# Attention and two feed-forward layers in one kernel: later pairs' keys and queries are transposed in the values' idle PSUM bank, and the way-in is reordered

## The chip, the cores and the metric

One core of a Trainium2 chip runs the whole program. The time is device microseconds of one execution, from its start to its end. TensorE (PE) multiplies matrices into PSUM, eight banks of 512 fp32 columns on 128 partitions; VectorE (DVE) and ScalarE (ACT) read PSUM; GpSimd (POOL) works from SBUF to SBUF; SyncE (SP) issues the DMAs. Each engine runs its own instructions in order and waits on semaphores.

## The reference

Inputs are q, k and v of 4 batches x 8 heads x 576 rows x 64 columns.

```
q, k = rotate(q), rotate(k)             # rotary embedding
attn = softmax(q @ k.T / sqrt(64))      # per head, 576 x 576
x    = (attn @ v)                       # heads side by side: 2304 x 512
x    = (sigmoid(x @ w_gate) * (x @ w_val)) @ w_out     # 512 -> 1536 -> 512
out  = elu(x @ w_in) @ w_out2                          # 512 -> 2048 -> 512
```

## The kernel before, in words

The 32 heads are taken one after the other, two heads being a *pair* (16 pairs). A head has a *slot* of `NSTEP` = 10 steps: five for the first 288 query columns (half a = 0), five for the second, each step being one block of keys (four of 128 rows and one of 64). In a step PE computes, in this order, the scores `s` of this block (two products, of high and low parts of fp32 numbers), up to two products `mt` whose row maxima belong to the head two slots later, and the product `pv` of exponentials `e` and values that is five steps old. So the values of a head's first half run in steps 5 to 9 of its slot, those of its second half (`pv_1`) in steps 0 to 4 of the next slot.

ACT takes the exponentials; DVE takes the maxima `MX` of each `mt`, subtracts the rounded part of the last block (`p<-s,p`, `low_part`) and copies the finished values `u` out of PSUM (`evacuate`). Once per head the maxima are joined (`MJ`), turned by PE (`mr`) and sent by DMA (`W<-row`) into the operands `W` of the next head.

PSUM has three rings of banks: `ps_mt` (3 banks, maxima), `ps_qk` (3 banks, scores and `mr`) and `ps_pv` (2 banks, values). The two banks of `ps_pv` go to the two halves of a head in turn, so the bank of `pv_1` is free from the copy of its values in the middle of a slot to step 0 of the next.

Keys and queries are prepared a few slots ahead, a pair at a time. POOL rotates them (`rope_ops`: `rk`, `rq`, and `rt`, the last 64 rows of both). `split` has PE transpose them into a PSUM tile `T`, ACT copy the rounded part (`hl<-T`, "high") and DVE subtract it from `T` (`hl<-T,hl`, "low"). `move` sends the parts by DMA into `W`.

The order is written by hand: `at(slot, step, fn)` puts work on an agenda. In the main loop the agenda of step h - 0.5 runs first, then scores, maxima and values of step h, then the agenda of step h. What a function emits there goes to the end of each engine's queue. For pair `pr` and `s0 = 2*pr`, keys of pair 4 and later are split in slot s0-5 (an odd slot), queries in slot s0-4 (an even one). In an odd slot no `mt` runs at steps 8 and 9; in an even one it does.

From slot 5 on, `split_w` converts the first weights of the feed-forward layers: a piece of it is pulled at steps 2 and 5 of each slot (lines 122 to 143: integer work on DVE, copies on ACT, differences on POOL).

`inverse` takes the reciprocal of the softmax sums in parts: sums to DRAM, back as 128 x 9 (`r<-d`), reciprocal on DVE, back to DRAM (`d<-r`), and out to 64 rows (`rb<-d`); `normalized` multiplies on POOL.

The feed-forward layers follow at 302 us and are not touched.

Of the kernel before, what the change touches and what calls it, by code (L numbers as in the profile page):

```python
# [9 lines left out]
F32 = mybir.dt.float32  # L10
F32R = mybir.dt.float32r
AF = mybir.ActivationFunctionType
ALU = mybir.AluOpType
# [7 lines left out]
def attention_moe_moe_kernel(  # L21
# [15 lines left out]
    nc = tc.nc  # L37
    B, H, S, D = q.shape
    P = 128
    NT, DM = out.shape  # L40
    NPAIR = B * H // 2
# [4 lines left out]
    SM = ST * P  # L46
    TL = S - SM
    HS = S // 2
    HM = SM // 2
# [136 lines left out]
    with ExitStack() as att:  # L186
# [10 lines left out]
        ps_mt = banks.enter_context(tc.tile_pool(name="ps_mt", bufs=3, space=bass.MemoryType.PSUM))  # L197
        ps_qk = banks.enter_context(tc.tile_pool(name="ps_qk", bufs=3, space=bass.MemoryType.PSUM))
        ps_pv = banks.enter_context(tc.tile_pool(name="ps_pv", bufs=2, space=bass.MemoryType.PSUM))
# [36 lines left out]
        first = [raw_p.tile([P, n, 2, D * n], F32, tag=nm, name=f"{nm}0") for nm, n in (("k", ST // 2), ("q", ST // 2))]  # L236
        raws["k", 0] = first[0].rearrange("p a h x -> p (a h x)").rearrange("p (h t d) -> p h t d", h=2, d=D)
        raws["q", 0] = first[1].rearrange("p a h x -> p (a h x)").rearrange("p (a h t d) -> p a h t d", a=2, h=2, d=D)
        for j in range(2):
            nc.sync.dma_start(  # L240
                out=raws["k", 0][:, j].rearrange("p t d -> p (t d)"),
# [3 lines left out]
                out=tab[:, 1 - j].rearrange("p t d -> p (t d)"),  # L245
                in_=rope_main[:, 1, 1 - j].rearrange("p t d -> p (t d)"),
            )
        for j, queue in enumerate((nc.sync, nc.scalar)):
            queue.dma_start(
                out=raws["q", 0][:, j].rearrange("p h t d -> p h (t d)"),  # L250
# [62 lines left out]
        def at(slot, step, fn, *args):  # L313
            agenda.setdefault(slot * NSTEP + step, []).append((fn, args))

        rot = {}
# [51 lines left out]

        parts = {}

        def split(pr, which, half, pool, tag, low=None):

            if which == "k" and half == 0:

                parts[pr] = hl_p.tile([P, 4, S], F32R, tag="hl", name=f"hl{pr}")
            tails = which == "k" and half == 1
            c0, n = half * HM, HM + (P if tails else 0)
            T = pool.tile([P, 512], F32, tag=tag, name=f"T{which}{pr}_{c0}")[:, 0:n]
            rows = [rot[pr, which][:, c // P] for c in range(c0, c0 + HM, P)] + ([rot[pr, "t"]] if tails else [])
            for j, r in enumerate(rows):  # L380
                nc.tensor.transpose(T[:, j * P : (j + 1) * P], r.rearrange("p h d -> p (h d)"), ident)  # L381
            c0 += 0 if which == "k" else S + TL
            hi, lo = (parts[pr][:, 2 * j : 2 * j + 2].rearrange("p w s -> p (w s)")[:, c0 : c0 + n] for j in range(2))
            high = lambda: nc.scalar.copy(hi, T)
            rest = lambda: nc.vector.tensor_tensor(out=lo, in0=T, in1=hi.bitcast(F32), op=ALU.subtract)
            if low is None:
                high()
                rest()
            else:
                slot, step = low  # L390
                at(slot, step - 1, high)
                at(slot, step, rest)

        def move(pr, ab):

# [24 lines left out]
        def bank(pr, key, pool, tag):  # L420
            if (pr, key) not in banks_of:
                banks_of[pr, key] = pool.tile([P, 512], F32, tag=tag, name=f"T{key[0]}{key[1]}_{pr}")
            return banks_of[pr, key]
# [26 lines left out]
        def high(pr, key):  # L450
            T, hi, lo = way_in[pr, key]
            nc.scalar.copy(hi, T)
# [141 lines left out]
        def values(i, h):  # L594


            a, t = divmod(h, ST + 1)
            pr, ab = divmod(i, 2)
            par = pr % 2
            c = slice(a * HS, (a + 1) * HS)  # L600
            if t == 0:
                ps[i, a] = ps_pv.tile([P, 512], F32, tag="pv", name=f"pv{i}_{a}")[:, 0:HS]
            out_ps = ps[i, a]
            e = probs.pop((i, h))
            if t == ST:
                nc.tensor.matmul(out_ps[0:D], lhsT=VT[par][:, ab, 0:D], rhs=e, start=False, stop=False)  # L606
                nc.tensor.matmul(out_ps, lhsT=VT[par][:, ab, D : 3 * D], rhs=e, start=False, stop=True)  # L607
            else:
                nc.tensor.matmul(out_ps, lhsT=VF[par][:, ab, t], rhs=e, start=t == 0, stop=False)  # L609
            if t < ST:  # L610
                return
            if ab == 0 and a == 0:
                us[pr] = (fin_p if pr == NPAIR - 1 else u_p).tile([P, S], F32, tag="u", name=f"u{pr}")
                sums[pr] = SUM[D * par : D * par + D]
            done = us[pr][D * ab : D * ab + D, c], sums[pr][32 * ab : 32 * ab + 1, c], out_ps
            if (i, a) == (NHEAD - 1, 1):
                return done
            at(i + 1, 5 * a + (0.5 if a else 3), evacuate, *done, "s")
            at(i + 1, 5 * a + 1, evacuate, *done, "u")

        def evacuate(u, total, out_ps, which="us"):
            if "u" in which:
# [6 lines left out]
        def inverse(pr, part):  # L629

            n = 2 * S // P
            spread = lambda x: x.rearrange("h s -> (h s)").rearrange("(p j) -> p j", p=P)
            if part == 0:
                dtmp[pr] = dram.tile([2, 2, S], F32, tag="d2", name=f"d2_{pr}"), (small_p if pr == NPAIR - 1 else s_p).tile([P, n], F32, tag="r", name=f"r{pr}")
            d2, r = dtmp[pr]
            if part == 0:
                nc.sync.dma_start(out=d2[0], in_=sums.pop(pr)[0 : D : D // 2])
            elif part == 1:
                nc.sync.dma_start(out=r, in_=spread(d2[0]))
            elif part == 2:  # L640
                nc.vector.reciprocal(r, r)
                nc.sync.dma_start(out=spread(d2[1]), in_=r)
            else:
                rb = dtmp[pr, "rb"] = fin_p.tile([P, S], F32, tag="rb", name=f"rb{pr}", bufs=1)
                for ab in range(2):
                    nc.sync.dma_start(out=rb[ab * D : (ab + 1) * D], in_=d2[1, ab : ab + 1].to_broadcast([D, S]))
# [29 lines left out]
        for par, ab in ((0, 0), (1, 1)):  # L676
            at(-6, 0, constants, par, ab, nc.gpsimd)
        for pr, which, eng in ((0, "k", nc.vector), (0, "q", nc.vector), (0, "t", nc.vector), (1, "k", nc.gpsimd), (1, "q", nc.gpsimd), (1, "t", nc.gpsimd)):
            gen = rope_ops(pr, which, eng)
            at(-6, 1, pull, gen, 4)  # L680
        at(-2, 0, first_pair)
# [10 lines left out]
        at(-1, 3, second_keys)  # L692
        at(-1, 4, low, 1, ("k", 1))
        at(-1, 6, zeros, 6, (0, ("q", 1)))
        at(0, 2, split_v, 0, 0, nc.scalar.copy)
        for half in range(2):
            at(0, 2 + half, second_queries, half)
        at(0, 3, split_v, 0, 1)
        at(0, 5, second_tails)
        at(0, 3.5, low, 1, ("q", 0))  # L700
        at(0, 4.5, low, 1, ("q", 1))
# [5 lines left out]
        for pr in range(NPAIR):  # L707
            s0 = 2 * pr
            if pr > 1:
                for j, (which, slot, steps) in enumerate(  # L710
                    (
                        ("k", *{2: (-1, (2, 2, 4, 4)), 3: (0, (10, 10, 11, 11))}.get(pr, (s0 - 6, (1, 3, 6, 8)))),
                        ("t", *{2: (-1, (6,) * 4), 3: (1, (2,) * 4)}.get(pr, (s0 - 6, (9,) * 4))),
                        ("q", *((0, (0, 0, 3, 3)) if pr == 2 else (s0 - 5, (1,3,6,8)))),
                    )
                ):
                    gen = rope_ops(pr, which, nc.gpsimd)
                    for st in steps:
                        at(slot, st, pull, gen)
                for j, (which, half) in enumerate((("k", 0), ("k", 1), ("q", 0), ("q", 1))):  # L720
                    slot, step = {2: ((0, 9), (0, 10), (1, 2), (1, 3)), 3: ((2, 1), (2, 2), (2, 4), (2, 7))}.get(
                        pr, ((s0 - 5, 3), (s0 - 5, 7), (s0 - 4, 3), (s0 - 4, 7))
                    )[j]
                    at(slot, step - 0.5, split, pr, which, half, ps_mt, "mt", (slot, step + 1))
                at(s0 - 4, 15 if pr == 2 else 9, move, pr, 0)
                at(s0 - 4, 15 if pr == 2 else 9, last_queries, pr, nc.gpsimd.tensor_copy)
                at(s0 - 4, 19, move, pr, 1)
            for piece in range(2 if pr > 0 else 0):
                at(s0 - 1, (5, 7)[piece], split_v, pr, piece)
        for pr in range(2, NPAIR):  # L730
            slot, step = {2: (-6, 1), 3: (-1, 7), 4: (1, 7)}.get(pr, (2 * pr - 8, 3))
# [3 lines left out]
            at(*{1: (-6, 1), 2: (1, 7)}.get(g, (4 * g - 8, 4)), load_tails, "kq", g, raw_p)  # L735
            at(4 * g - 2, 3, load_v, g)
        for pr in range(NPAIR):
            for part, step in enumerate((7, 12, 18, 23)):
                at(2 * pr + 2, step, inverse, pr, part)
            for seg in range(4):  # L740
                at(2 * pr + 2, 30 + seg, normalized, pr, seg)

        def first_tokens():
            prep.close()
# [17 lines left out]
        for n in range(-6 * NSTEP, NHEAD * NSTEP + half_slot):  # L762
            i, h = divmod(n, NSTEP)
# [10 lines left out]
            if 0 <= i < 3:  # L774
                first = NSTEP // 2 - i % 2
# [16 lines left out]
        rest = remaining()  # L792
# [111 lines left out]
    done, before = 0, None  # L904
    for c in range(NCH):
# [3 lines left out]
        done = 0  # L909
# [64 lines left out]
```

## Time and profile before

| | us |
|---|---|
| median of three runs | 1146.98 (1146.27 to 1147.35) |
| the profiled execution, its own time | 1147.52 |
| its span | 1145.7 |
| PE busy | 1135.5 |
| DVE, POOL, ACT busy | 901.2, 608.5, 455.5 |
| way-in, to 27 us: PE busy | 21.91 of 27 |
| attention, 27 to 302 us: PE busy | 274.25 of 275 |
| feed-forward, 302 us to the end: PE busy | 839.34 of 844 |

A busy PE is not PE at its peak: the ends of matmuls are modelled, and one that waits a little for a semaphore still shows as busy time or as a later start. Starts of neighbouring matmuls, compared with the same place in another slot, show such waits. The granted clock of TensorE is 1.00 in each of the three stretches.

### The profile page before, as it was taken

The numbers are of one execution on the slowest core, as the hardware profiler recorded it, in microseconds if no ns is written. First come the engines' busy times: TensorE is split into PE (matmuls) and PEld (weight loads), VectorE is DVE, ScalarE is ACT, GpSimd is POOL, SyncE is SP. The second block draws the span as 40 slices with busy tenths as digits, with TensorE's granted clock in tenths as the row PEclk, the third lists the DMA queues.
The fourth block names the chain that finished last, engine by engine and source line by source line (L and its number), as shares of the span: only waits on it lengthen the run. The fifth ranks groups of instructions, "written<-read, shape, count | busy, mean of one in ns | idle before, by whom it ended". The sixth has DMA issues, their size and how long they took to land.

```text
span 1145.7 us, 16891 instructions
## 1 busy us (share of the span) xinstructions
PE 1135.5 (99%) x5783; PEld 964.2 (84%) x5783; DVE 901.2 (79%) x1860; ACT 455.5 (40%) x1048; POOL 608.5 (53%) x695
## 2 busy tenths in 40 slices
PE   8999999999999999999999999999999999999998
PEld 7888888888888888888888888888888888888887
DVE  8789888988587977777676666888999999999744
ACT  6667767677644322212122223344322222322221
POOL 8858676772455544444444435766554555545321
PEclk9999999999999999999999999999999999999999
DMA  7886867764131211111111110111111111110004
GB/s 184 195 216 150 199 164 180 179 152 112 41 103 37 74 39 54 37 42 52 38 55 38 36 55 19 37 37 56 37 50 44 37 56 37 56 37 1 1 37 129
DMA packets 59718, 88.93 MB, mean 78 GB/s; under 512 B 18304, under 2 KB 31632, under 8 KB 59632
## 3 DMA queue, kind: packets, MB, share of 16 engines
q1 hardware_dynamic: 58912, 87.32, 28.6%
q8 instruction: 46, 0.75, 0.3%
q10 hardware_dynamic: 720, 0.52, 0.1%
q14 instruction: 40, 0.33, 0.1%
HBM read 55.45 MB, written 4.87 MB: 53 GB/s over the span
## 4 chain that ended last, share of the span: by engine, by line
PE 96%; POOL 1%; DMA 1%; DVE 1%; issue 0%; SPq 0%; ACT 0%; DVEq 0%; POOLq 0%
PE h L814 14%; PE h L815 14%; PE h L813 14%; PE pv L609 10%; PE o L813 10%; PE o L814 10%; PE o L815 10%; PE s L580 7%; PE mt L534 3%; PE pv L606 1%; PE pv L607 1%; PE Tk L381 1%; PE Tq L381 1%; DMA W<-row 0%; DMA r<-d 0%
## 5 line engine op out<-in xcount | busy, mean ns | idle before, releaser
L845 POOL TENSOR_TENSOR gl<-g,gh 128x512 fp32r<-128x512 f32 (+1 forms) x140 | 169.3, 1209 | 348.5 <-ACT gh L844 241.3
L844 ACT CAST gh<-g 128x512 fp32r<-128x512 f32 (+1 forms) x140 | 81.0, 579 | 263.0 <-DVE g L834 139.6
L580 PE MATMUL s<-W 128*128 128x288 f32 (+1 forms) x640 | 179.7, 361 | 0.9 <-ACT e L587 0.6
L814 PE MATMUL h<-xl,wh 128*128 128x512 f32 (+1 forms) x480 | 176.6, 368 | 0.0
L813 PE MATMUL h<-xh,wh 128*128 128x512 f32 (+1 forms) x480 | 176.6, 368 | 0.0
L815 PE MATMUL h<-xh,wl 128*128 128x512 f32 (+1 forms) x480 | 176.5, 368 | 0.0
L609 PE MATMUL pv<-e,VF 128*128 128x288 f32 x512 | 165.3, 405 | 0.3 <-ACT SUM L625 0.3
L141 POOL TENSOR_TENSOR ca<-ca,wh 128x256 f32<-128x256 f32 x136 | 110.8, 815 | 69.5 <-DVE cm L135 47.1
L536 DVE TENSOR_REDUCE MX<-mt 128x1 f32<-128x288 f32 x288 | 126.4, 449 | 26.9 <-PE mt L534 25.5
L587 ACT ACTIVATE e<-s 128x288 f32<-128x288 f32 x256 | 105.0, 412 | 67.5 <-PE s L580 65.0
L136 ACT CAST wh<-ca 128x256 fp32r<-128x256 f32 x136 | 55.1, 405 | 187.5 <-DVE ca L132 187.4
L580 PEld LDWEIGHTS s<-W 128*128 128x128 f32 (+1 forms) x640 | 104.2, 179 | 24.8 <-ACT e L587 1.7
L834 DVE TENSOR_TENSOR g<-h,g 128x512 f32<-128x512 f32 (+1 forms) x60 | 38.2, 637 | 105.7 <-PE h L815 103.2
L143 POOL TENSOR_TENSOR wl<-ca,cm 128x256 fp32r<-128x256 f32 x136 | 112.0, 823 | 17.6 <-DVE cm L138 12.2
L814 PE MATMUL h<-yl,wh 128*128 128x512 f32 (+1 forms) x320 | 117.7, 368 | 0.0
L815 PE MATMUL h<-yh,wl 128*128 128x512 f32 (+1 forms) x320 | 117.7, 368 | 0.0
L813 PE MATMUL h<-yh,wh 128*128 128x512 f32 (+1 forms) x320 | 117.7, 368 | 0.0
L813 PE MATMUL o<-wh,gh 128*128 128x512 f32 x290 | 112.6, 388 | 0.5 <-DVE z L898 0.5
L814 PE MATMUL o<-wl,gh 128*128 128x512 f32 x290 | 112.5, 388 | 0.0
L815 PE MATMUL o<-wh,gl 128*128 128x512 f32 x290 | 112.4, 387 | 0.0
L813 PEld LDWEIGHTS h<-xh,wh 128*128 128x128 f32 x480 | 90.5, 189 | 15.2
L815 PEld LDWEIGHTS h<-xh,wl 128*128 128x128 f32 x480 | 90.5, 189 | 15.0
(136 smaller groups left out, 2486.4 us busy)
## 6 DMA issues: line engine op xcount, KB each, us to landing
W<-hl SPq DMA_DIRECT2D x93, 288.0 KB
raw<-in_moe_w_out_dram SPq DMA_DIRECT2D x28, 512.0 KB
raw<-in_moe_w_in_dram SPq DMA_DIRECT2D x16, 512.0 KB
raw<-in_moe_w_gate_dram SPq DMA_DIRECT2D x12, 512.0 KB
raw<-in_moe_w_val_dram SPq DMA_DIRECT2D x12, 512.0 KB
rb<-d SPq DMA_DIRECT2D x32, 144.0 KB
v<-in_v_dram SPq DMA_DIRECT2D x8, 512.0 KB
k<-in_k_dram SPq DMA_DIRECT2D x15, 256.0 KB
```

What stands on the lines that cost most here:

```text
L136: nc.scalar.copy(h, a)
L141: nc.gpsimd.tensor_tensor(out=a, in0=a, in1=h.bitcast(F32), op=ALU.subtract)
L143: nc.gpsimd.tensor_tensor(out=l, in0=a, in1=mf, op=ALU.add)
L536: nc.vector.tensor_reduce(out=MX[pr % 2][:, a, c : c + 1], in_=m, axis=AX.X, op=ALU.max, negate=True)
L580: nc.tensor.matmul(s, lhsT=operand(i, st, t * P, n), rhs=operand(i, mv, a * HS, HS), start=st == "K1", stop=st == "K2")
L587: nc.scalar.activation(e, s, AF.Exp, scale=SCALE)
L609: nc.tensor.matmul(out_ps, lhsT=VF[par][:, ab, t], rhs=e, start=t == 0, stop=False)
L813: nc.tensor.matmul(ps, lhsT=ah, rhs=bh, start=j == 0, stop=False)
L814: nc.tensor.matmul(ps, lhsT=ah, rhs=bl, start=False, stop=False)
L815: nc.tensor.matmul(ps, lhsT=al, rhs=bh, start=False, stop=j == n - 1)
L844: nc.scalar.copy(hi, g)
L845: nc.gpsimd.tensor_tensor(out=lo, in0=g, in1=hi.bitcast(F32), op=ALU.subtract)
```

## The change

For pairs 4 and later a pair had four splits of 256 columns (keys with the tails' 128 more in the second), all in the ring `ps_mt`, at steps 2.5 and 6.5 of the two slots. Now it has three pieces: the tails (128 columns, `ps_mt`, step 6.5 of the keys' slot), the keys as one bank of 512 columns in the ring `ps_pv` at step 7.5 of that slot, and the queries likewise at step 7.5 of the next. High parts are copied half a step after the transposes, low parts one step later; `move` is put half a step later. Pairs 2 and 3 have three pieces in `ps_mt`, pair 3's earlier than before. `u` of `pv_1` is copied at step 5.5 instead of 6. The reciprocal goes to step 21 of its 40 instead of 18, the DMA `d<-r` to a part of its own at step 22, `rb` to 27. At the way-in the first pair's values are copied by POOL instead of ACT and before the tails' rotation, the tails of the values (`VT`) two steps and more sooner, and pair 2's tails are rotated after its queries.

```diff
-        def split(pr, which, half, pool, tag, low=None):
+        def split(pr, piece, ring, slot, step):
...
+            which, first, last = PIECES[piece]
+            rows = [] if which == "t" else [rot[pr, which][:, j] for j in range(first, last)]
+            rows += [rot[pr, "t"]] if piece in ("t", "k1") else []
+            n = P * len(rows)
+            T = ring[0].tile([P, 512], F32, tag=ring[1], name=f"T{piece}_{pr}")[:, 0:n]
...
-                at(slot, step - 1, high)
-                at(slot, step, rest)
+            at(slot, step, nc.scalar.copy, hi, T)
+            at(slot, step + 1, lambda: nc.vector.tensor_tensor(out=lo, in0=T, in1=hi.bitcast(F32), op=ALU.subtract))
...
-            at(i + 1, 5 * a + (0.5 if a else 3), evacuate, *done, "s")
-            at(i + 1, 5 * a + 1, evacuate, *done, "u")
+            at(i + 1, 5 * a + (0.5 if a else 2), evacuate, *done, "s")
+            at(i + 1, 5.5 if a else 1, evacuate, *done, "u")
...
                 nc.vector.reciprocal(r, r)
+            elif part == 3:
                 nc.sync.dma_start(out=spread(d2[1]), in_=r)
...
+            if (pr, which) == (1, "t"):
+                at(-6, 1, split_v, 0, 0)
...
-        at(0, 2, split_v, 0, 0, nc.scalar.copy)
+        at(-1, 5, split_v, 0, 1)
...
-        at(0, 3, split_v, 0, 1)
...
-                        ("t", *{2: (-1, (6,) * 4), 3: (1, (2,) * 4)}.get(pr, (s0 - 6, (9,) * 4))),
-                        ("q", *((0, (0, 0, 3, 3)) if pr == 2 else (s0 - 5, (1,3,6,8)))),
+                        ("t", *{2: (0, (4,) * 4), 3: (1, (2,) * 4)}.get(pr, (s0 - 6, (9,) * 4))),
+                        ("q", *{2: (0, (0, 0, 3, 3)), 3: (1, (1, 3, 4, 4))}.get(pr, (s0 - 5, (1, 3, 6, 8)))),
...
-                    slot, step = {2: ((0, 9), (0, 10), (1, 2), (1, 3)), 3: ((2, 1), (2, 2), (2, 4), (2, 7))}.get(
-                        pr, ((s0 - 5, 3), (s0 - 5, 7), (s0 - 4, 3), (s0 - 4, 7))
-                    )[j]
-                    at(slot, step - 0.5, split, pr, which, half, ps_mt, "mt", (slot, step + 1))
-                at(s0 - 4, 15 if pr == 2 else 9, move, pr, 0)
+                mt, pv = (ps_mt, "mt"), (ps_pv, "pv")
+                for piece, ring, slot, step in {
+                    2: (("k", mt, 0, 10), ("q", mt, 1, 3), ("t", mt, 1, 4)),
+                    3: (("k", mt, 2, 1), ("t", mt, 2, 2), ("q", mt, 2, 3)),
+                }.get(pr, (("t", mt, s0 - 5, 7), ("k", pv, s0 - 5, 8), ("q", pv, s0 - 4, 8))):
+                    at(slot, step - 0.5, split, pr, piece, ring, slot, step)
+                at(s0 - 4, 15.5 if pr == 2 else 9.5, move, pr, 0)
...
-            for part, step in enumerate((7, 12, 18, 23)):
+            *steps, first = (7, 12, 21, 22, 27, 33) if pr < NPAIR - 2 else (7, 12, 18, 18, 23, 30)
```

What this makes of the order on the engines is shown at three places. The first is PE from step 7.5 of slot 7 to step 1 of slot 8, where pair 6's keys are transposed (the number after a tile's name is a running one, that before it the step). Before:

```order
L609 MATMUL pv_0_1507<-e_2_1460,VF_167 128x288
L580 MATMUL s_8_1541<-W_165 128x288 x2
L609 MATMUL pv_0_1507<-e_3_1475,VF_167 128x288
L580 MATMUL s_9_1550<-W_165 64x288 x2
L606 MATMUL pv_0_1507<-p_4_1487,VT_169 64x288
L607 MATMUL pv_0_1507<-p_4_1487,VT_169 128x288
L580 MATMUL s_0_1561<-W_162 128x288 x2
L534 MATMUL mt_0_1565<-W_164 128x288
L609 MATMUL pv_1_1568<-e_5_1499,VF_167 128x288
```

and now:

```order
L606 MATMUL pv_0_1489<-e_2_1446,VF_167 128x288
L385 MATMUL Tk_1521<-ident,rk_1281 128x128 x4
L577 MATMUL s_8_1527<-W_165 128x288 x2
L606 MATMUL pv_0_1489<-e_3_1458,VF_167 128x288
L577 MATMUL s_9_1535<-W_165 64x288 x2
L603 MATMUL pv_0_1489<-p_4_1469,VT_169 64x288
L604 MATMUL pv_0_1489<-p_4_1469,VT_169 128x288
L577 MATMUL s_0_1547<-W_162 128x288 x2
L531 MATMUL mt_0_1551<-W_164 128x288
L606 MATMUL pv_1_1554<-e_5_1481,VF_167 128x288
```

`Tk_1521` and `pv_1_1554` lie in the same bank: the transposes wait for DVE's copy of the values that were there, and `pv_1_1554` waits for DVE's low part of `Tk_1521`.

The second is DVE over the same steps, from the `low_part` of step 5.5 on. Before:

```order
L590 TENSOR_TENSOR p_4_1487<-s_4_1488,p_4_1487 64x288
L536 TENSOR_REDUCE MX_170<-mt_6_1518 128x1
L623 COPY u_1417<-pv_1_1436 64x288
L536 TENSOR_REDUCE MX_170<-mt_7_1533 128x1
L641 RECIPROCAL r_1393<-r_1393 128x9
L385 TENSOR_TENSOR hl_1471<-Tk_256_1524,hl_1471 128x384
L536 TENSOR_REDUCE MX_171<-mt_0_1565 128x1
```

and now:

```order
L587 TENSOR_TENSOR p_4_1469<-s_4_1470,p_4_1469 64x288
L620 COPY u_1404<-pv_1_1424 64x288
L533 TENSOR_REDUCE MX_170<-mt_6_1501 128x1
L533 TENSOR_REDUCE MX_170<-mt_7_1514 128x1
L389 TENSOR_TENSOR hl_1506<-Tt_1507,hl_1506 128x128
L389 TENSOR_TENSOR hl_1506<-Tk_1521,hl_1506 128x512
L533 TENSOR_REDUCE MX_171<-mt_0_1551 128x1
```

The copy `u` stands one maximum sooner, the low part is that of the whole bank, and the reciprocal has left this place.

The third is POOL at the way-in, from the end of pair 1's queries on. Before:

```order
L366 TENSOR_TENSOR rq_221<-rq_221,sq_222 128x512
L362 TENSOR_TENSOR st_227<-kq_140,tabt 128x128
L364 TENSOR_TENSOR rt_226<-kq_140,tabt 128x128
L366 TENSOR_TENSOR rt_226<-rt_226,st_227 128x128
L362 TENSOR_TENSOR sk_371<-k_231,tab 128x2x4x64
L364 TENSOR_TENSOR rk_370<-k_231,tab 128x2x4x64
L366 TENSOR_TENSOR rk_370<-rk_370,sk_371 128x512
L362 TENSOR_TENSOR st_388<-kq_235,tabt 128x128
```

and now:

```order
L366 TENSOR_TENSOR rq_221<-rq_221,sq_222 128x512
L405 COPY VF_166<-v_149 128x8x64
L362 TENSOR_TENSOR st_228<-kq_140,tabt 128x128
L364 TENSOR_TENSOR rt_227<-kq_140,tabt 128x128
L366 TENSOR_TENSOR rt_227<-rt_227,st_228 128x128
L362 TENSOR_TENSOR sk_372<-k_232,tab 128x2x4x64
L364 TENSOR_TENSOR rk_371<-k_232,tab 128x2x4x64
L366 TENSOR_TENSOR rk_371<-rk_371,sk_372 128x512
L409 TENSOR_TENSOR VT_168<-vv_151,VT_168 64x2x64
```

The copy of the values is ahead of the tails' rotation, and the difference for `VT` comes right after pair 2's keys; before it stood after pair 2's tails and two thirds of its queries.

## Rows read from the trace of the kernel before

**Rows 1.** The page: engines' busy time, share and instructions.
```profile
PE 1135.5 (99%) x5783; PEld 964.2 (84%) x5783; DVE 901.2 (79%) x1860; ACT 455.5 (40%) x1048; POOL 608.5 (53%) x695
```
**Rows 2.** Waits of PE: line, releaser, us in total, times, longest.
```profile
PE s L580 <- ACT e L587: 0.6, 1, 0.6
```
**Rows 3.** PE in order of time, end of slot 22: start, us, line, tiles, shapes, count.
```profile
225.41 0.30 PE L534 MATMUL mt<-hl,QT 128*128 128x288 f32 x1
225.80 0.43 PE L580 MATMUL s<-W 128*128 128x288 f32 x2
226.20 0.65 PE L609 MATMUL pv<-e,VF 128*128 128x288 f32 x2
```
**Rows 4.** DVE in order of time, there.
```profile
225.34 0.43 DVE L385 TENSOR_TENSOR hl<-Tq,hl 128x256 fp32r<-128x256 f32 x1
225.74 0.46 DVE L536 TENSOR_REDUCE MX<-mt 128x1 f32<-128x288 f32 x1
```
**Rows 5.** DVE and ACT by shape: count, busy us, mean ns, idle before.
```profile
L456 DVE TENSOR_TENSOR hl<-Tk,hl 128x512 fp32r<-128x512 f32 x1 | 0.7, 668 | 0.0
L452 ACT CAST hl<-Tk 128x512 fp32r<-128x512 f32 x1 | 0.6, 587 | 1.1 <-PE Tk L431 1.1
```
**Rows 6.** PE in order of time, end of slot 21 (and a wait at 291 us).
```profile
215.12 0.64 PE L580 MATMUL s<-W 128*128 128x288 f32 x2
...
217.00 0.65 PE L609 MATMUL pv<-e,VF 128*128 128x288 f32 x2
...
291.37 0.72 PE L609 MATMUL pv<-e,VF 128*128 128x288 f32 x2 [0.31 <-ACT SUM L625]
```
**Rows 7.** ACT in order of time, ends of slots 21 and 22.
```profile
215.80 0.41 ACT L587 ACTIVATE e<-s 128x288 f32<-128x288 f32 x1
...
223.84 0.41 ACT L587 ACTIVATE e<-s 128x288 f32<-128x288 f32 x1 [0.38 <-PE s L580]
224.14 0.37 ACT L384 CAST hl<-Tq 128x256 fp32r<-128x256 f32 x1
```
**Rows 8.** DVE in order of time, steps 5 to 8 of slot 21.
```profile
213.35 1.30 DVE L125 TENSOR_SCALAR cm<-raw 128x256 int32<-128x256 int32 x1
214.68 0.45 DVE L590 TENSOR_TENSOR p<-s,p 64x288 fp32r<-64x288 f32 x1
215.42 0.44 DVE L623 COPY u<-pv 64x288 f32<-64x288 f32 x1
```
**Rows 9.** DVE by shape, 54 to 262 us: the pieces pulled at step 5.
```profile
L132 DVE SCALAR_TENSOR_TENSOR ca<-ce,cm 128x256 f32<-128x256 int32 x7 | 6.2, 892 | 0.0
L138 DVE SCALAR_TENSOR_TENSOR cm<-raw,cm 128x256 f32<-128x256 uint32 x7 | 5.4, 769 | 0.0
L125 DVE TENSOR_SCALAR cm<-raw 128x256 int32<-128x256 int32 x7 | 4.2, 605 | 0.0
```
**Rows 10.** Line 125 alone: shortest, median and longest in ns.
```profile
L125 DVE TENSOR_SCALAR cm<-raw x7: 274/635/1300, 78.5 to 240.9; 128x256 int32<-128x256 int32 x7
```
**Rows 11.** POOL in order of time, steps 5 to 8 of slot 21.
```profile
213.22 1.28 POOL L364 TENSOR_TENSOR rq<-q,tab 128x512 f32<-128x512 f32 x1
```
**Rows 12.** PE in order of time, way-in.
```profile
19.14 0.40 PE L534 MATMUL mt<-hl,W 128*128 128x288 f32 x1 [0.29 <-ACT W L467]
...
26.56 0.35 PE L606 MATMUL pv<-p,VT 128*64 128x288 f32 x1 [1.57 <-POOL VT L412]
```
**Rows 13.** POOL in order of time, way-in.
```profile
20.86 1.28 POOL L366 TENSOR_TENSOR rk<-rk,sk 128x512 f32<-128x512 f32 x1
...
26.05 0.45 POOL L412 TENSOR_TENSOR VT<-vv,VT 64x128 fp32r<-64x128 f32 x1
```
**Rows 14.** ACT in order of time, way-in.
```profile
17.44 0.61 ACT L408 COPY VF<-v 128x512 f32<-128x512 f32 x1
```
**Rows 15.** DVE in order of time, the reciprocal at 163 us.
```profile
163.21 0.22 DVE L641 RECIPROCAL r<-r 128x9 f32<-128x9 f32 x1 [1.92 <-DMA r<-d]
```
**Rows 16.** PE in order of time, slot 23, a wait for operands.
```profile
235.08 0.40 PE L580 MATMUL s<-W 128*128 128x288 f32 x1 [0.20 <-DMA W<-row]
```

More of the change, by code (lines that the diff above doesn't have):

```diff
@@ L369, in attention_moe_moe_kernel @@
         parts = {}
-        def split(pr, which, half, pool, tag, low=None):
-            if which == "k" and half == 0:
+        PIECES = {"k": ("k", 0, 4), "q": ("q", 0, 4), "t": ("t", 0, 0)}
+        PIECES |= {f"{w}{j}": (w, 2 * j, 2 * j + 2) for w in "kq" for j in range(2)}
+        def split(pr, piece, ring, slot, step):
+            if pr not in parts:
                 parts[pr] = hl_p.tile([P, 4, S], F32R, tag="hl", name=f"hl{pr}")
[L376 to L379, printed above, removed]
+            which, first, last = PIECES[piece]
[3 more added lines that the diff above has]
+            T = ring[0].tile([P, 512], F32, tag=ring[1], name=f"T{piece}_{pr}")[:, 0:n]
             for j, r in enumerate(rows):
                 nc.tensor.transpose(T[:, j * P : (j + 1) * P], r.rearrange("p h d -> p (h d)"), ident)
-            c0 += 0 if which == "k" else S + TL
+            c0 = {"k": 0, "t": SM, "q": S + TL}[which] + first * P
             hi, lo = (parts[pr][:, 2 * j : 2 * j + 2].rearrange("p w s -> p (w s)")[:, c0 : c0 + n] for j in range(2))
[L384 to L390, printed above, removed]
-                at(slot, step - 1, high)
-                at(slot, step, rest)
+            at(slot, step, nc.scalar.copy, hi, T)
+            at(slot, step + 1, lambda: nc.vector.tensor_tensor(out=lo, in0=T, in1=hi.bitcast(F32), op=ALU.subtract))
         def move(pr, ab):
@@ L719, in attention_moe_moe_kernel @@
                         at(slot, st, pull, gen)
-                for j, (which, half) in enumerate((("k", 0), ("k", 1), ("q", 0), ("q", 1))):
-                    slot, step = {2: ((0, 9), (0, 10), (1, 2), (1, 3)), 3: ((2, 1), (2, 2), (2, 4), (2, 7))}.get(
-                        pr, ((s0 - 5, 3), (s0 - 5, 7), (s0 - 4, 3), (s0 - 4, 7))
-                    )[j]
-                    at(slot, step - 0.5, split, pr, which, half, ps_mt, "mt", (slot, step + 1))
-                at(s0 - 4, 15 if pr == 2 else 9, move, pr, 0)
-                at(s0 - 4, 15 if pr == 2 else 9, last_queries, pr, nc.gpsimd.tensor_copy)
+                mt, pv = (ps_mt, "mt"), (ps_pv, "pv")
[5 more added lines that the diff above has]
+                at(s0 - 4, 15.5 if pr == 2 else 9.5, move, pr, 0)
+                at(s0 - 4, 15.5 if pr == 2 else 9.5, last_queries, pr, nc.gpsimd.tensor_copy)
                 at(s0 - 4, 19, move, pr, 1)
@@ L737, in attention_moe_moe_kernel @@
         for pr in range(NPAIR):
-            for part, step in enumerate((7, 12, 18, 23)):
+            *steps, first = (7, 12, 21, 22, 27, 33) if pr < NPAIR - 2 else (7, 12, 18, 18, 23, 30)
+            for part, step in enumerate(steps):
                 at(2 * pr + 2, step, inverse, pr, part)
             for seg in range(4):
-                at(2 * pr + 2, 30 + seg, normalized, pr, seg)
+                at(2 * pr + 2, first + seg, normalized, pr, seg)
         def first_tokens():
```

## The prediction

> **What bounds the kernel now.** I read the page first, then the waits of PE, then PE, DVE and ACT in order of time at the slots' ends, and last the groups by shape. The page gives PE 1135.5 us of busy time, 99% of the span [rows 1]. The reader is to see that nothing is won here by making DVE or ACT shorter, only by PE's waits, and that any new wait of PE is paid in full, since it has no idle time in which to catch up. The waits of PE are few, and those of the attention that the change can touch are small: 0.6 us for an exponential [rows 2], and the ones named under the way-in below. So the forecast hangs on whether the change makes PE wait at new places. The change leaves PE's own products as they were: the same number of 128x128 transposes and of 128x288 products. It changes what must have happened before two of them may start: the first `pv_1` of a slot, which lies now in the bank that the transposes used, and the transposes, which need the copy `u` to have emptied that bank.
>
> There are 12 pairs with the new split (4 to 15), so 12 slot ends with keys and 12 with queries.
>
> **Term 1, queries, even to odd slot.** `pv_1` follows the last two maxima and the first scores. In slot 22 the maximum of step 9 runs on PE at 225.41, the next slot's scores at 225.80 and `pv_1` at 226.20 [rows 3]. DVE's order puts the low part, moved to step 9, behind `MX` of that step, which starts at 225.74, 0.33 after its product [rows 4]. DVE starts one such operation about 0.37 after the other (two of them lie between 214.68 and 215.42 [rows 8]), so the low part starts at 226.11. It is 128x512; at the way-in the same shape took 0.668 [rows 5]; it ends at 226.78. From the end of an operation to the PE product that waits for it go 0.06 (`VT` ends at 26.50 [rows 13], its product starts at 26.56 [rows 12]), so `pv_1` may start at 226.84 and waits 0.64. A product pair after a wait takes 0.72 instead of 0.65 [rows 6], which makes 0.71. Times 12: **8.5 us**. Behind the waiting `pv_1` stand all of PE's products, so nothing takes this up.
>
> **Term 2, keys, odd to even slot.** Here DVE is idle before the low part, since no maxima run at steps 8 and 9; ACT decides. The high part is queued behind the exponential of step 8. In slot 21 the scores of step 8 start at 215.12 [rows 6], their exponential at 215.80, and the next ACT operation follows an exponential by 0.30 (223.84 to 224.14) [rows 7]: the high part starts at 216.10. As 128x512 it took 0.587 [rows 5] and ends at 216.69; 0.06 to DVE, 0.668 for the low part, 0.06 to PE: 217.48. `pv_1` was at 217.00 [rows 6], so it waits 0.48, with the restart 0.55. Times 12: **6.6 us**.
>
> Bounds of the two together. Below: operations in a row overlap by up to 0.1 at their ends (0.41 long, the next 0.30 later [rows 7]); if each of the copies gives that, 0.5 and 0.3 are left, 9.6 us. Above: one more DVE operation of 0.37 ahead of the low part of the keys, and 0.1 for the queries, 0.81 and 0.92, 20.8 us. I take 15.1, by the rows of the very shape.
>
> **Term 3, the transposes wait for `u`.** They stand at step 7.5 ahead of the scores of step 8, so with four products at about 0.06 each PE wants to start them 0.23 before 215.12 [rows 6], at 214.89. `u` stands now right behind `low_part`, and that behind the weights' piece pulled at step 5. In slot 21 this piece (line 125) took 1.30, and `low_part` started at 214.68 [rows 8]; `u` then starts 0.37 later, at 215.05, lasts 0.44 and lets PE go at 215.55: a wait of 0.67. So a slot loses what its piece takes beyond 0.63. The pieces at step 5 are of three lines, 605, 892 and 769 ns in the mean over seven each [rows 9], together 755 over 21 slots. The least loss is that of the mean, 21 x 0.125 = 2.6 us. But the pieces scatter: line 125 alone goes from 274 to 1300 ns [rows 10]. Were all of them either 0.27 or 1.30, 47% would be long and the loss 21 x 0.47 x 0.67 = 6.6; were all long, 14. I take **4 us**.
>
> What makes a piece long is seen in slot 21: POOL's `rq` of 1.28 us begins at 213.22 [rows 11] and the piece lasts until `rq` is about done. The Trainium skill ("SBUF — State Buffer", section "Who interferes with whom") says that DVE and GpSimd share one pair of SBUF ports under an exclusive lock, and that an instruction which needs the pair while the other engine holds it fully blocks; the trace agrees here, with 1.30 us beside POOL's 1.28. By that rule a piece is late whenever POOL is in a rotation, and term 3 goes towards its upper end; the row on line 125 says that it isn't so in every slot. That end is the third rival below.
>
> **Term 4, way-in.** PE waited 1.57 us for `VT` and 0.29 for ACT's `W` [rows 12]. `VT` now comes right after pair 2's keys, which end at 22.14 [rows 13]; POOL does the values' copy before that. How long it takes there no row shows; ACT's took 0.61 [rows 14], and a POOL operation on as many elements 1.28 [rows 13], so `VT` ends between 23.2 and 23.9, ahead of 24.99, where PE wanted it. ACT has 0.61 less to do, which takes off its two waits (0.29, and 0.57 of the exponential [rows 2]). The sum is **-2.4 us**; 0 if the next thing, the DMAs of the operands, is late by as much.
>
> **Term 5, DMA waits in the stage.** DVE's reciprocal waited 1.92 us for its DMA [rows 15], and maxima behind it came late; at step 21 instead of 18 it has 2.7 us more. SP no longer stands at `d<-r` ahead of an operand's transfer, for which PE waited 0.20 [rows 16]. Bounds: -0.2, if three banks of maxima covered the reciprocal, and -2.1, if nothing did. I take **-1.6**. Pair 2's and 3's new places I cost at nothing: they use the same ring, one slot is relieved and another is filled; 0.8 either way.
>
> **Sum.** 1147.5 (the profiled execution's own time) + 8.5 + 6.6 + 4 - 2.4 - 1.6 = 1162.6. This execution was 0.5 above the median, so 1162.1; I say **1162.0 us**, 1.3% slower.
>
> **Rivals.** *A, faster:* the bank is read out before it is wanted, and the 24 slot ends cost nothing. This turns on one point: the low part must end by 226.14 in the queries' slot, so start by 225.47, which is before the last maximum's own start [rows 4]; and in the keys' slot the chain over ACT would have to be 0.48 shorter than its two copies' 1.26 allow. For it speaks that DVE and ACT have idle time on the whole (79% and 40% busy [rows 1]); against it that both chains hang on PE's own last products, and idle time earlier doesn't help them. It leaves the gains, 1147.5 - 2.4 - 1.6 - 0.5 = 1143.0, or up to 1146 with term 3's least. *B, only one kind of end waits:* if ACT gets the high part of the keys out sooner than its queue says, or the scores in front of `pv_1` start later anyway, term 2 is gone and the time is about 1155.5. For it speaks that its wait is the smaller one and made of three short handovers; against it that all its durations stand in rows. *C, every piece at step 5 is long:* term 3 is 14 instead of 4, the time about 1172. For it: `u` now lies nearer to the piece, and POOL has a rotation in most odd and even slots alike; against it line 125's shortest 274 ns, and means below 0.9 us. *D, no change in effect:* the gains at the way-in and in the stage are as forecast and the ends cost a third of my terms each, 1148 to 1150.
>
> **How the numbers follow.** Forecast 0.68, its own range 1153 to 1171 (terms 1 and 2 from 9.6 to 20.8, term 3 from 2.6 to 6.6, the gains from 0.2 to 4.5); A 0.06; B 0.12; C 0.09; D 0.05. The range that holds 8 in 10 leaves out A, part of D and the outer part of C: 1150 to 1171. A difference under 0.2%, some 2.3 us, is what a measurement of this kernel can't tell from no change. Faster takes A and a little of D, 0.07; same is most of the rest of D, 0.04; slower 0.89.
>
> **What would show it.** In the changed kernel's profile the waits of PE have to show `pv` released by DVE's low part, about 24 times and some 0.5 to 0.65 us each, with the queries' ends the longer; PE's starts at a slot's end are then 0.7 later against the neighbours than here. The transposes `Tk` and `Tq` wait for DVE's copy `u` in slots 6 to 26, up to 0.7, and most where POOL runs `rq` or `rk` beside the piece. The wait for `VT` at 26 us is gone. The stretch from 302 us on takes the same 844 us, only later. I am wrong if `pv_1` starts right behind the maximum in most slots (then A), if the waits at the slots' ends stand at the queries only (B), or if the reordered way-in makes PE wait longer than the 2.4 us that it saves.

## The result, and the profile after

The changed kernel takes 1164.06 us (1163.68 to 1164.52, four runs) against 1146.88 us of the kernel before in the same series: ratio 1.0146, 95% interval 1.0134 to 1.0159. By the medians it is slower by 17.2 us. The forecast was 1162.0 and slower, the main case. The granted clock of TensorE is 1.00 in each of the three stretches, as before.

PE's waits, of after: line, releaser, us in total, times, longest. `s`, `mt`, `pv` and `u` stand three lines higher up than before (L577, L531, L606, L620); the transposes are on L385, the low part on L389, and the high part on L784, the line that runs the agenda.

```profile
PE 1140.8 (98%) x5783; PEld 965.0 (83%) x5783; DVE 897.4 (77%) x1846; ACT 452.5 (39%) x1033; POOL 608.7 (52%) x696
```

```profile
PE pv L606 <- DVE hl L389: 11.6, 23, 0.7
PE idle L439 <- DVE MJ L784: 1.6, 1, 1.6
PE mt L531 <- DVE MX L533: 1.1, 2, 0.6
PE Tk L385 <- DVE u L620: 1.0, 3, 0.5
PE o L814 <- DVE z L899: 0.5, 1, 0.5
PE mt L531 <- DMA W<-hl: 0.4, 1, 0.4
```

The first line did not exist before. It answers to the first named sign: 23 waits of `pv` for the low part, with 11.6 us of idle time alone (0.70 at a queries' end, 0.30 at a keys' end; counted from starts, as below, the delays are larger). The 1.6 us for `VT` [rows 12] are gone, and those of `Tk` for `u` are new.

A queries' end (even to odd slot, as [rows 3, 4]) in PE's, DVE's and ACT's order of time, of after:

```profile
239.16 0.30 PE L531 MATMUL mt<-hl,QT 128*128 128x288 f32 x1
...
239.57 0.42 PE L577 MATMUL s<-W 128*128 128x288 f32 x2
239.83 0.29 PE L531 MATMUL mt<-W 128*128 128x288 f32 x1
240.83 0.72 PE L606 MATMUL pv<-e,VF 128*128 128x288 f32 x2 [0.70 <-DVE hl L389]
```

```profile
239.50 0.46 DVE L533 TENSOR_REDUCE MX<-mt 128x1 f32<-128x288 f32 x1 [0.42 <-PE mt L531]
239.99 0.69 DVE L389 TENSOR_TENSOR hl<-Tq,hl 128x512 fp32r<-128x512 f32 x1
```

```profile
238.80 0.58 ACT L784 CAST hl<-Tq 128x512 fp32r<-128x512 f32 x1
```

The high part is there at 239.38, but DVE's low part stands behind the maximum of step 9 and starts at 239.99. `pv` starts 1.00 after the `mt` in front of it, where the undisturbed distance is about 0.13 (`pv` is 0.40 after the first scores in [rows 3], and `mt` here 0.26 after them): 0.87 late, and the pair's second product another 0.08.

A keys' end (odd to even slot, as [rows 6, 7, 8, 11]), of after, first PE, then DVE, ACT and POOL:

```profile
228.32 0.63 PE L385 MATMUL Tk<-ident,rk 128*128 128x128 f32 x4 [0.16 <-DVE u L620]
228.71 0.51 PE L577 MATMUL s<-W 128*128 128x288 f32 x2
...
230.06 0.43 PE L577 MATMUL s<-W 128*128 128x288 f32 x2
230.33 0.29 PE L531 MATMUL mt<-W 128*128 128x288 f32 x1
230.92 0.75 PE L606 MATMUL pv<-e,VF 128*128 128x288 f32 x2 [0.29 <-DVE hl L389]
```

```profile
226.21 1.12 DVE L125 TENSOR_SCALAR cm<-raw 128x256 int32<-128x256 int32 x1
227.36 0.45 DVE L587 TENSOR_TENSOR p<-s,p 64x288 fp32r<-64x288 f32 x1
227.74 0.44 DVE L620 COPY u<-pv 64x288 f32<-64x288 f32 x1
...
230.17 0.69 DVE L389 TENSOR_TENSOR hl<-Tk,hl 128x512 fp32r<-128x512 f32 x1 [0.94 <-ACT hl L784]
```

```profile
229.25 0.41 ACT L584 ACTIVATE e<-s 128x288 f32<-128x288 f32 x1 [0.91 <-PE s L577]
229.56 0.58 ACT L784 CAST hl<-Tk 128x512 fp32r<-128x512 f32 x1
```

```profile
225.90 1.28 POOL L366 TENSOR_TENSOR rq<-rq,sq 128x512 f32<-128x512 f32 x1
```

Here DVE waits 0.94 for ACT, whose high part stands behind the exponential of step 8. `pv` starts 0.59 after its `mt`: 0.46 late, and the second product another 0.10. The slot also shows term 3: the piece (line 125) runs beside `rq` and takes 1.12, `u` ends at 228.18, and the transposes wait.

### The profile page after: what moved, and what is told of

Its sections match the earlier page's. It is cut to its first block, busy times and chain, and to the rows that moved or that the text cites. A ratio compares the mean times of both kernels' runs of the same rounds, so it can differ in the third digit from the quotient of the medians.

```text
span 1162.4 us, 16867 instructions
## 1 busy us (share of the span) xinstructions
PE 1140.8 (98%) x5783; PEld 965.0 (83%) x5783; DVE 897.4 (77%) x1846; ACT 452.5 (39%) x1033; POOL 608.7 (52%) x696
## 4 chain that ended last, share of the span: by engine, by line
PE 93%; DVE 4%; DMA 1%; ACT 1%; issue 0%; DVEq 0%
PE h L816 14%; PE h L814 14%; PE h L815 14%; PE pv L606 10%; PE o L814 10%; PE o L815 10%; PE o L816 10%; PE s L577 6%; PE mt L531 3%; DVE hl L389 1%; DVE MX L533 1%; DMA W<-hl 1%; PE Tq L385 1%; PE Tk L385 1%; ACT e L584 1%; ACT hl L784 0%
## 5 line engine op out<-in xcount | busy, mean ns | idle before, releaser
L577 PE MATMUL s<-W 128*128 128x288 f32 (+1 forms) x640 | 180.9, 363 | 0.4 <-ACT e L584 0.4
L606 PE MATMUL pv<-e,VF 128*128 128x288 f32 x512 | 167.3, 409 | 11.6 <-DVE hl L389 11.6
L577 PEld LDWEIGHTS s<-W 128*128 128x128 f32 (+1 forms) x640 | 105.2, 179 | 26.6 <-ACT e L584 1.3
L815 PEld LDWEIGHTS h<-xl,wh 128*128 128x128 f32 x480 | 90.5, 189 | 15.1
```

The lines of the kernel that those rows point to most:

```text
L577: nc.tensor.matmul(s, lhsT=operand(i, st, t * P, n), rhs=operand(i, mv, a * HS, HS), start=st == "K1", stop=st == "K2")
L815: nc.tensor.matmul(ps, lhsT=ah, rhs=bl, start=False, stop=False)
```

## The experiments

Each ratio is against the kernel before in the same series, and what a run gains on the changed kernel is worked out from the two ratios. e1, e2, e3, e5 and e6 stand alone on the changed kernel; e4 joins e2 and e3; b1_all joins e4, e5 and e6; b2_v and b3_q_later stand on b1_all, b4_row_act and b5_move_later on b3_q_later. From `e3` on the lines are four more than after's where the edit adds lines.

**e1_halves.**

```diff
-                }.get(pr, (("t", mt, s0 - 5, 7), ("k", pv, s0 - 5, 8), ("q", pv, s0 - 4, 8))):
+                }.get(pr, (("k0", mt, s0 - 5, 3), ("k1", mt, s0 - 5, 7), ("q0", mt, s0 - 4, 3), ("q1", mt, s0 - 4, 7))):
```

> The changed kernel with one part undone: pairs 4 to 15 are split again in four halves in the ring ps_mt, at the steps of the kernel before; way-in, pairs 2 and 3, the sooner copy u and the later reciprocal stay. Theory (the loss is the shared bank: 11.6 us of waits of pv_1 for DVE's low part, and 6 or so of the slow restarts and of a later release behind them, 18.0 in starts of PE; 1.9 of transposes that wait for u): all of it goes, 1164.1 - 19.9 = 1144.2; what stays is the gain in the stage and the little of the way-in, so it is faster than before by some 2.5 us. Rival (the stage's gain of 2.5 comes because maxima no longer share their ring with transposes): that gain goes too, 1146.7, the same as before. In both, no wait of pv_1 for a low part is left.

Measured: 1.0003 (0.9993 to 1.0012), the same as before. The whole loss goes with the bank; no wait of `pv` for a low part is left. Nothing of the rest of the change is a gain in sum, as the rival's number has it, but not by the rival's cause: the transposes share the maxima's ring again, and still the even slots 10, 12, 16, 18, 22 and 26, where no DMA is late, take 8.91 to 8.95 us, against 9.01 to 9.79 in the kernel before. The trace shows what took the gain, operands that come late in slots 4, 8, 20 and 24, most of it a row of maxima:

```profile
PE s L577 <- DMA W<-row: 2.0, 2, 1.3
```

**e2_low_first.** DVE's low part ahead of the maximum of step 9.

```diff
-            at(slot, step + 1, lambda: nc.vector.tensor_tensor(out=lo, ...))
+            at(slot, step + (0.5 if pr > 3 and piece in ('k', 'q') else 1), lambda: ...)
```

> The changed kernel; for the whole-bank pieces of pairs 4 to 15 DVE's low part is queued half a step sooner, ahead of the maximum of step 9. Theory (queries' ends: DVE's queue decides, since the high part ended at 141.56 and the low part could have started at 141.60 instead of 142.18; keys' ends: ACT decides): pv_1 at the queries' ends is let go 0.55 sooner, 12 x 0.55 = 6.6 us, 1157.5; the keys' ends are as they were, pv_1 0.85 after the slot's first scores. Rival (at the queries' ends the second thing that pv_1 waits for, PE's own transposes or the way its wait is given out, holds it, as its release 0.14 behind the low part hints): under 2 us, 1162 to 1164.

Measured: 1.0084 (1.0067 to 1.0101), 7.1 us less than the changed kernel. At the queries' ends `pv` comes 0.68 after the first scores instead of 1.26, at the keys' ends 0.85 as it was. The theory holds; DVE's queue was the cause there.

**e3_high_first.** ACT's high part ahead of the exponential of step 8.

```diff
-            at(slot, step, nc.scalar.copy, hi, T)
+            early = pr > 3 and piece in ('k', 'q')
+            if early:
+                nc.scalar.copy(hi, T)
+            else:
+                at(slot, step, nc.scalar.copy, hi, T)
```

> The changed kernel; ACT's high part of the whole-bank pieces is queued right behind the transposes, ahead of the exponential of step 8. Theory: in the keys' slots the high part starts at the transposes' end, some 0.5 sooner, and the low part with it; pv_1 doesn't wait there (0.39 after the slot's first scores instead of 0.85, and no slow second product), 12 x 0.57 = 6.8 us, 1157.3. At the queries' ends nothing changes, since the low part stays behind the maximum of step 9. Rival (the exponential, now 0.3 later, makes the scores' ring late): half of it comes back as waits of s for ACT's e, 1160 to 1161.

Measured: 1.0082 (1.0067 to 1.0097), 7.3 us less. At the keys' ends `pv` is at 0.39, undisturbed, but for pair 4's (0.75); at the queries' ends at 1.26, unchanged. PE's waits name only the queries' ends now, 12 of them:

```profile
PE pv L610 <- DVE hl L393: 8.5, 12, 0.7
```

**e4_both_first.** Both edits.

> The changed kernel with both edits: high part ahead of the exponential of step 8, low part ahead of the maximum of step 9. Theory: with both ends' copies sooner the bank is read out before pv_1 wants it; all 18 us of the ends go, 1146 (the transposes' 1.9 of waiting for u stays), the same as before within 0.2%. More than the two edits' sum by themselves (6.6 + 6.8 = 13.4), since at the queries' ends the low part alone still ends 0.26 too late by ACT's high part. Rival (the edits gain no more than their sum): 1150.7.

Measured: 1.0014 (1.0004 to 1.0023), 15.1 us less than the changed kernel, between the two numbers. In the trace the theory's part is met: no wait for a low part is left, and `pv` stands at 0.39 at 21 of the 24 ends; at the other three (slots 4, 8 and 20) the score or the maximum in front of it waits for a DMA. Two things are seen of the 3 us that are missing. At the 12 queries' ends the pair's second product still comes 0.30 to 0.31 behind the first instead of 0.24, 0.8 in all, though the first is on time. And rows of maxima land late; the two slots with these waits are together 3.3 us longer than their like. The profiled execution, 1150.25, was the second slowest of ten, so the median one has lost less to them.

```profile
PE s L581 <- DMA W<-row: 2.3, 2, 1.2
```

```profile
92.49 0.40 PE L581 MATMUL s<-W 128*128 128x288 f32 x1 [1.13 <-DMA W<-row]
```

**e5_u_first.**

```diff
-            at(i + 1, 5 * a + (0.5 if a else 2), evacuate, *done, "s")
-            at(i + 1, 5.5 if a else 1, evacuate, *done, "u")
+            at(i + 1, 5 if a else 2, evacuate, *done, "s")
+            at(i + 1, 4.5 if a else 1, evacuate, *done, "u")
```

> The changed kernel; the copy u of pv_1 is queued at step 4.5 instead of 5.5, ahead of the maximum and the weights' piece of step 5 (the row of sums half a step sooner too). Theory (the transposes wait for u because the piece stands in front of it, 1.9 us in starts of PE, of which 0.65, 0.47 and 0.32 in three slots): no transpose of a whole bank waits for u any more, 1164.1 - 1.9 = 1162.2. Rival (DVE, held in front of u until pv_1 is through, makes the maxima behind it late and PE waits for their banks): as much comes back, 1164 to 1165.

Measured: 1.0124 (1.0111 to 1.0138), 2.5 us less than the changed kernel. No transpose waits for `u` any more, and nothing came back on the maxima. The theory holds in its cause; whether the gain is more than its 1.9, the intervals don't tell.

**e6_soon23.** For pairs 2 and 3 alone, the high part right behind the transposes and the low part at `step` instead of `step + 1`.

> The changed kernel; for pairs 2 and 3 alone the high parts are queued right behind the transposes and the low parts a step sooner. Theory (the 2.5 us won at the way-in are lost again in slot 1 because two of the three banks of maxima are held by transposes whose copies are a step late: maxima wait 0.71, 0.56, 0.23 and 0.19 there, and 0.68 in slot 2): most of these 2.4 us go, 1162.0. Rival (POOL's rotation of pair 2's queries, which is no sooner than before, is what slot 1 waits for, and the wait shows at the transposes instead): under 0.5 us, 1163.6 to 1164.1.

Measured: 1.0141 (1.0126 to 1.0157), 0.6 us less, which the two intervals don't tell from nothing. The trace says more: slot 1 did get shorter, from 11.19 to 9.83 us, but slot 2 grew from 10.19 to 11.24, since pair 3's queries are not yet rotated:

```profile
38.52 0.66 PE L385 MATMUL Tq<-ident,rq 128*128 128x128 f32 x4 [1.00 <-POOL rq L366]
```

```profile
37.20 1.26 POOL L366 TENSOR_TENSOR rq<-rq,sq 128x512 f32<-128x512 f32 x1
```

So theory and rival are each half right: the banks made slot 1 late, and POOL, one slot on, was next.

**b1_all.** The edits of e4, e5 and e6 together.

> All four edits on the changed kernel: high parts right behind the transposes, low parts ahead of the maximum (a step sooner for pairs 2 and 3), u at step 4.5. By the sum: 1148.5 (both copies first) - 1.9 - 2.4 = 1144.2, 0.23% faster than before. Rival (what is late next takes it: the operands' row, whose DMA is queued behind the moves and for which PE waited 2.3 us in the kernel with both copies first, grows as the slots get shorter): 1146.5, the same as before.

Measured: 0.9984 (0.9975 to 0.9993), 1145.61 us in the median of 11 runs (1144.19 to 1146.66), faster than the kernel before by 0.16% (0.07% to 0.25%). That is the sum's direction, but under the 0.2% that the forecast took as the bound. It is, by the ratios, 18.6 us faster than the changed kernel, with the same bank for the transposes. Its profiled execution, 1144.19, is the fastest of the eleven, so its trace, with one wait for a row (0.2 us), need not stand for the others.

**b2_v.** The values' load at step 0 instead of 3 of its slot.

> As the kernel with all four edits, and the loads of the values three steps sooner. Theory (SP stands at a move's DMA until the values' load of 5 to 8 us has landed, at 88.39 in the kernel with both copies first, and the row is queued behind it): the waits of PE for W<-row go, 2.3 us less than the kernel with all four edits, 1142. Rival (the row lands late because the rings of the DMA engines are full with weights, keys and queries, whatever the order): no difference from that kernel.

Measured: 1.0012 (1.0003 to 1.0020), slower than b1_all by 0.28%. Theory and rival both missed: the waits for `W<-row` became more, not fewer. Why the sooner load does that was not tried.

```profile
PE s L581 <- DMA W<-row: 2.0, 5, 0.7
```

**b3_q_later.** Pair 3's queries are split at `("q", mt, 2, 5)` instead of `("q", mt, 2, 3)`.

> The kernel with all four edits, and pair 3's queries transposed two steps later in slot 2 (step 4.5). Theory (their transposes wait 1.1 us for POOL's rotation, which ends at 38.42, and 1.3 in starts of PE; two steps later they find it done): 1.2 us less than the kernel with all four edits, whose ratio to the kernel before was 0.9984; so 0.9974, 1143.9. Rival (the queries' parts reach the operands later, and the maxima of slot 4 wait for that DMA, as they did 0.4 us in the changed kernel, or a bank held at step 5 makes slot 2's maxima wait): no gain, 1145.

Measured: 0.9987 (0.9979 to 0.9996), 1145.68 us: no gain over b1_all. The wait for `rq` is gone and slot 2 is shorter by 0.8 us, but the profiled execution, one in the middle of its eleven, loses 1.6 us to rows. Whether that is more than b1_all loses in such an execution isn't shown, since the trace of b1_all is of its fastest.

**b4_row_act.** In `max_row` the three DMAs are issued by ACT (`nc.scalar.dma_start`).

> As the kernel with pair 3's queries later, and the rows of maxima are sent to the operands from ACT's queue instead of SP's. Theory (a row is late, up to 1.3 us of wait of PE in one place, because SP issues it behind a move's DMAs and stands there): no wait of PE for W<-row is left, and the runs scatter less; the time is that of the kernel with pair 3's queries later or up to 2 us less. Rival (ACT, held in front of a row's DMA until DVE has made the row, makes its exponentials late): PE waits for ACT in each slot instead, 32 times some 0.1 to 0.5 us, 1148 to 1160.

Measured: 1.0171 (1.0158 to 1.0185), the rival's cause, and at 1166.81 us dearer than its 1148 to 1160. No wait for a row is left; PE waits for ACT in its place, 0.7 to 0.9 us about the middle of each even slot from 4 to 28, and three times elsewhere.

```profile
PE s L581 <- ACT e L588: 12.0, 16, 0.9
```

**b5_move_later.**

```diff
-                at(s0 - 4, 15.5 if pr == 2 else 9.5, move, pr, 0)
+                at(s0 - 4, 15.5 if pr == 2 else 9.5 if pr == 3 else 12.5, move, pr, 0)
```

> As the kernel with pair 3's queries later, and the first move of pairs 4 to 15 three steps later, behind the next head's row instead of ahead of it on SP. Theory (every fourth slot SP has some ten DMAs to issue in 6 us, at about 0.6 each; the row, issued at 86.59 behind three of a move, landed at 90.20, just when PE wants it, and in other executions later): the row is issued some 2 us sooner, no wait of PE for W<-row is left in any slot, 1.6 us less than the kernel with pair 3's queries later: ratio 0.9973, some 1143.5, and less scatter. Rival (the moved parts are now what is late: maxima two slots on wait for the DMA W<-hl): no gain or slower, 1145 to 1150.

Measured: 1.0189 (1.0175 to 1.0202), the rival's cause, and at 1169.04 us far above its 1145 to 1150. The row is in time but for one wait; the moved parts are late for all 12 pairs:

```profile
PE mt L535 <- DMA W<-hl: 18.5, 12, 2.8
...
PE s L581 <- DMA W<-row: 0.4, 1, 0.4
```

## Why the prediction was right, and where its terms were off

The account of the attention is made from starts of PE's products, against the same neighbours elsewhere in the same kernel; the first scores of slot 28 start at 287.28 instead of 270.28, 17.0 us later, and from there on nothing more is lost (the spans differ by 16.7).

| term | forecast | measured |
|---|---|---|
| 1, queries' ends | 8.5 | 12 x (0.87 + 0.08) = 11.3 |
| 2, keys' ends | 6.6 | 11 x (0.46 + 0.10) = 6.3, and 0.8 at the twelfth, where a DMA decides (below) |
| 3, transposes wait for `u` | 4 | 1.9 in eight slots |
| 4, way-in | -2.4 | -2.5, of which 2.1 are lost again in slot 1: -0.4 |
| 5, stage | -1.6 | -2.9, the remainder |

The mechanism was right: the places, the engines that decide, and the sign. That the sum, 15.1, is only 1.9 short is in part luck. Against the forecast, the ends came out 3.3 dearer (0.8 of it by a late DMA) and the way-in's gain 2.0 less, while term 3 was 2.1 cheaper and the stage's gain 1.3 more. The range is not the sum of the bounds that it names either: from 1147.0 they give 1154.7 to 1174.2, not 1153 to 1171.

**Terms 1 and 2** are shown: e2 shortens the queries' ends and e3 takes away the keys', each leaving the other as it was, and e4 takes both. The places, the engine that decides at each, and the number of waits came as forecast. Term 2's wait of 0.48 was measured as 0.46, restart 0.07 as 0.10. Term 1 was mis-sized by 0.23 a slot: DVE's low part starts 0.49 after the maximum's start (239.50 to 239.99), not the 0.37 that was read from two other operations in a row [rows 8], and `pv` follows its end by 0.15 (240.68 to 240.83), not 0.06. At the keys' ends that step takes 0.06 (230.86 to 230.92), the size read from the way-in. What the two places differ in is that `pv` waits at the queries' ends on two semaphores (DVE's and PE's own) and at the keys' ends on one; that this costs the 0.09 was not tried, and stays open. e2 excludes the maximum as its cause, since `pv` came 0.15 behind the low part there as well. Nor is the second product's 0.08 at the queries' ends a restart after the wait: in e4 and b1_all `pv` starts on time and 0.06 to 0.07 of it stay. At the keys' ends the 0.10 goes with the wait.

At the twelfth keys' end, pair 4's, `mt` waits 0.4 us for the DMA `W<-hl` of pair 3 just ahead of `pv`, which covers the low part. The 0.8 us come without the shared bank too: in e1 `pv` is as late there (1.21 after the first scores instead of 0.39). In e6, where pairs 2 and 3 are read out sooner, it stands at 0.85 like the other keys' ends, so the rest is one more cost of these pairs' new places.

**Term 3** was right in kind and too big. The threshold read as 0.63 is 0.79 in the keys' slots (pieces of 0.96, 1.12, 1.27 and 1.45 gave waits of 0.16, 0.32, 0.47 and 0.66), and only five of the 21 pieces, the shortest of them 0.87, passed it; three queries' slots lost 0.07 each at pieces of 0.65. The pieces are also shorter than before, 0.62 us in the mean instead of 0.755, since they fall otherwise beside POOL. Their length follows POOL closely. Line 125 takes 0.28 to 0.29 where no POOL operation runs, 0.47 beside shorter operations, and 0.96 and 1.12 beside a rotation; beside a rotation it ends 0.15 to 0.16 after it (in slot 21 the rotation ends at 227.18, the piece at 227.33). That agrees with what the prediction cited from the Trainium skill ("SBUF — State Buffer", section "Who interferes with whom"): the blocked instruction stops until the other is through. It is why rival C, each piece long, did not come: a piece pays only what is left of the operation that it meets, and 8 of the 21 met none. e5 took 2.5 us away by moving `u` out of the pieces' way.

**Term 4** came as forecast up to slot 1; what failed is the sentence under term 5 that costs pair 2's and 3's new places at nothing. The gain first: `VT` is done at 23.19 and slot 1 starts 2.53 us sooner.

```profile
22.73 0.46 POOL L409 TENSOR_TENSOR VT<-vv,VT 64x128 fp32r<-64x128 f32 x1
```

```profile
29.83 0.40 PE L531 MATMUL mt<-W 128*128 128x288 f32 x1 [0.55 <-DVE MX L533]
...
31.47 0.37 PE L531 MATMUL mt<-W 128*128 128x288 f32 x1 [0.29 <-DVE hl L389]
```

Then maxima wait in slot 1, because pair 2's queries and tails hold two of the three banks of maxima until 31.32 and 32.53, and slot 1 takes 11.19 us instead of 9.08. e6 showed the cause and what is behind it: POOL's rotations are no sooner than before, so a front part that is 2.5 us ahead meets them one slot on. In e6 slot 1 is still 0.75 longer than in the kernel before; what that is, no run shows.

**Term 5** was too small. 17.0 less the other rows leaves -2.9. Where it lies shows in the lengths of the slots: in the kernel before the even slots 6 to 26 take 8.95 to 9.79 us, 3.4 more in sum than 8.91 each, the length of an undisturbed one in e1. In after they take 9.49 to 9.60, of which 0.57 is term 2, so 0.5 of the 3.4 is left. The forecast counted one wait of DVE for `r<-d`; the kernel before has five, about the starts of slots 12, 14, 16, 20 and 24 (DVE's waits, of before):

```profile
DVE r L641 <- DMA r<-d: 5.3, 5, 1.9
```

After and e1 have none. The two longest, 1.92 and 1.68 us, are in slots 16 and 24, the slots that are most too long (0.88 and 0.77); slot 24 has the wait for the row too (that of [rows 16], which stands in its first step). e1 keeps this gain in the slots where no DMA is late, so it does not come from the ring. No run undoes the later reciprocal alone, so its share is not shown apart from the other new places on SP. A slower slot gives each DMA more time, so part of the gain on rows may belong to the loss itself.

Rivals A, B and D are refuted by the 23 waits and by the two kinds of ends in the trace.

## What to carry to other kernels

A bank that is idle in the middle of a period is free only if its guest has been *read out* before the owner returns: count the chain product, copy, difference, release, each behind what its engine's queue puts in front, not the mean load of the engines. Here DVE and ACT are idle a fifth and three fifths of the time, and still cost 18 us; two changes of queue order, an operation of 0.4 us each, gave nearly all of it back. Where the tensor engine is never idle, each wait is paid in full, and each gain is passed on to the next thing that is just in time: here POOL's rotations, then DMAs.

## What the runs showed of the hardware beyond the forecast

- At the keys' ends a wait costs twice: the pair's second product comes 0.10 late as well, and no more where e3 takes the wait away. At the queries' ends it comes 0.08 late with the wait and still 0.06 to 0.07 without it (e4, b1_all); the cause is open.
- The release of PE behind DVE's end took 0.06 at one place and 0.15 at another, constant over all slots.
- DMAs that are just in time are the next limit here: in b5_move_later three steps' delay of a move (some 2.7 us) cost 18.5 us in 12 waits. Rows cost 0.2 to 2.3 us in the kernels of 1144 to 1150 us, different in each, and next to nothing in the slower after, e3 and e6. No kernel was reached that is fast and waits for no row.
- Line 125's pieces that begin while a rotation runs on POOL, two in after, end 0.15 to 0.16 after the rotation does.
